# A router and eight experts behind sigmoid attention: the second expert product in row form, one comparison input in PSUM, gathered row blocks turned six transposes at a time

## The chip, the core and the metric

The kernel runs on one core of a Trainium2 chip. A core has five engines that run side by side, each through its own list of instructions in order: TensorE (PE, matrix products and transposes; PEld is its weight load), VectorE (DVE), ScalarE (ACT), GpSimd (POOL) and SyncE (SP, which issues most transfers). TensorE writes only to PSUM, a small accumulator memory of eight banks; the engines wait for each other by semaphores. The metric is device time of one execution in microseconds (us), the median of several runs.

## What is computed

Attention with a sigmoid in place of the softmax, then a layer of eight experts in which each expert takes exactly 448 of the 3584 tokens, chosen greedily by the largest gate values:

```python
def _attn_ref(q, k, v):                      # 8 batches, 12 heads, 448 positions, 64 wide
    scores = scale * np.matmul(q, k.transpose(0, 1, 3, 2)) - np.log(S)
    return np.matmul(1.0 / (1.0 + np.exp(-scores)), v)

def _moe_ref(x, w_gate, w1, w2):             # x: 3584 x 768, 8 experts, hidden 1024
    cap = N // E                             # 448
    order = np.argsort(-(x @ w_gate).flatten())
    for idx in order:
        tok, e = (int(idx) // E, int(idx) % E)
        if assigned[tok] >= 0 or counts[e] >= cap:
            continue
        assigned[tok] = e
        counts[e] += 1
    for e in range(E):
        mask = assigned == e
        out[mask] = np.maximum(x[mask] @ w1[e], 0.0) @ w2[e]
```

All of it is fp32. A product that must keep fp32 accuracy is made of three matmuls: each factor is split into a rounded part (`h`, type fp32r) and the rest (`l`), and the sum takes h x h, h x l and l x h.

## The kernel before

**Stages.** Up to some 276 us the attention runs. To about 327 us the router finds the first expert's tokens while the attention rows `xs` are written to memory. From there the eight experts run one after the other, in the order in which the router finds them full; while one expert is computed, the router (on DVE, with small matmuls on TensorE) finds the tokens of the next.

**One expert** (`moe(kx)`). Its 448 token rows are fetched by an indirect transfer into `xg`, in four row blocks of 128, 128, 128 and 64 (`gather`). Each row block is turned by TensorE so that the model dimension lies on the partitions: two half turns of three 128x128 transposes into a `tp` bank of PSUM, from where ACT makes the rounded part `xh` and DVE the rest `xl` (`xturn`). There are two `tp` buffers.

The first product makes the hidden layer transposed: four blocks `i` of 256 hidden units, each 36 matmuls with 448 moving columns (the tokens) into one `sc` accumulator. An `sc` is two PSUM banks, and there are two of them. ACT reads it twice, as the rounded part `hh` and as fp32 `yt`, and POOL subtracts the two into `hl`.

The second product also comes out transposed: three slices `i` of 256 output columns, each 48 matmuls of 448 columns into one `sc` (L716, L718, L720). A weight block is the stationary operand, the hidden layer moves. ACT copies the result to `yt`, and for each of the four token blocks `untranspose` (L642) turns it back: two transposes into a `tp` bank (L646), a copy of 256 columns into the row buffer `yr` (L651), and after the third slice an indirect transfer on POOL that scatters the rows to `out` (L654). In the last expert the last slice is computed in two cuts of 256 and 192 columns.

**Weights.** `units` lists the weight pieces in order. For each, SP loads `wr`, ACT makes the rounded part `wh` and POOL (for odd pieces from `W_DVE` on, DVE) the rest `wl`. `stream(u)` at the start of piece u issues the load three pieces ahead and the split two ahead. There are four buffers of each.

**What sets the order.** The program is written out in one order by hand: `moe` is a generator that yields after each matmul its estimated cost (`MM` = 189 ns), and the loop around it adds these up in `clock`. When the clock passes a router step's due time the next piece of the router is issued; otherwise, at most every `CHORE_NS` = 1000 ns, the first chore that is due: a gather, a half turn or a back-turn. So the distance between chores is counted in matmuls. What is left at the end of an expert is issued at once (`flush`). The times of the clock decide the order only; each engine then runs its list as its waits allow.

**The router's lists.** `lists` builds from each token's slot number a table of 64 x 32 comparisons a partition (`oh`, L279), which TensorE uses 32 times (L284) to turn slots into token numbers. Both inputs, `io64` and `rr`, are 16-bit integers in SBUF.

## Time and profile before

| what | time |
|---|---|
| median of 3 runs | 883.82 us (882.51 to 1052.58) |
| the profiled execution | 882.62 us |
| its span, from the first instruction to the last | 880.8 us |
| PE busy | 836.0 us (95%) |
| PE weight loads busy | 639.6 us (73%) |
| DVE, ACT, POOL busy | 530.4, 455.3, 467.2 us |
| chain that ended last: PE, DVE, waits on issue | 79%, 10%, 4% |
| transfers | 117.57 MB, mean 133 GB/s |

The profile is of one execution. Its span is 1.8 us shorter than its own time, and that time is close to the lower end of the runs. The chain is the work that ended last, followed back from the last instruction; TensorE's share of it says that the time is mostly a row of its instructions. A row of the timeline gives the start and the length in us, the engine, the line, the operation and what it writes and reads; a row of the groups gives the busy time of all, the mean of one in ns, and the idle time before it with what ended it.

### The profile page before, as it was taken

To read this page: it belongs to the slowest core of one execution; us is meant where nothing else is said; L and a number is where in the kernel's file an instruction comes from. 1 tells how busy PE (TensorE), PEld (TensorE's weight loads), DVE (VectorE), ACT (ScalarE), POOL (GpSimd) and SP (SyncE) were. 2 spreads that over 40 slices of the span, in tenths; PEclk is the share of its full clock that TensorE was granted. 3 is DMA by queue.
4 is the path that set the end of the run, shared out by engine and by line. 5 is a ranking of instruction groups with operands and counts; after the bars stand their busy time and mean duration, and the time that the engine had idled before them with its cause. 6 is when DMAs were issued, how large, how long until landed. Compare 5 with 4: busy or idle time off the path is not lost.

```text
span 880.8 us, 16227 instructions
## 1 busy us (share of the span) xinstructions
PE 836.0 (95%) x5507; PEld 639.6 (73%) x5507; DVE 530.4 (60%) x2045; ACT 455.3 (52%) x611; POOL 467.2 (53%) x449
## 2 busy tenths in 40 slices
PE   6999999999998739998999999999999999999996
PEld 3455455455455629987988988988888888889996
DVE  4665555555555978868779789779699521421110
ACT  6777777777775714334435434434434434544431
POOL 9645444444400025846854964974873882752641
PEclk9999999999999959999999999999999999999998
DMA  9876666666603954334543543452452442722511
GB/s 174 170 142 127 132 124 124 128 127 122 136 19 121 325 178 128 102 115 155 144 135 109 168 138 108 143 161 93 141 165 94 155 147 73 243 98 75 192 48 63
DMA packets 203507, 117.57 MB, mean 133 GB/s; under 512 B 143936, under 2 KB 193088, under 8 KB 203424
## 3 DMA queue, kind: packets, MB, share of 16 engines
q1 hardware_dynamic: 190688, 83.03, 36.0%
q0 software_dynamic: 10880, 33.28, 12.0%
q8 instruction: 43, 0.70, 0.3%
q10 hardware_dynamic: 1856, 0.23, 0.2%
q14 instruction: 40, 0.33, 0.1%
HBM read 94.47 MB, written 22.02 MB: 132 GB/s over the span
## 4 chain that ended last, share of the span: by engine, by line
PE 79%; DVE 10%; issue 4%; POOL 3%; DMA 3%; ACT 0%; ACTq 0%; SPq 0%; POOLq 0%; DVEq 0%
PE tp L462 13%; PE sc L438 11%; PE sc L683 9%; PE sc L681 8%; PE sc L685 8%; PE sc L718 6%; PE sc L720 6%; PE sc L716 6%; DVE r_junk L173 4%; PE tp L468 2%; PE sc L448 2%; PE tp L646 2%; DMA xr<-xs,r_idx 2%; PE tp L633 2%; PE tp L483 1%
## 5 line engine op out<-in xcount | busy, mean ns | idle before, releaser
L599 POOL TENSOR_TENSOR wl<-wr,wh 128x768 fp32r<-128x768 f32 (+1 forms) x96 | 205.8, 2152 | 135.6 <-ACT wh L597 128.3
L428 ACT ACTIVATE at<-sc,bias 128x896 f32<-128x896 f32 x168 | 161.0, 1005 | 63.3 <-PE sc L448 38.4
L373 POOL DMA_DIRECT2D nkq<-in_q_dram x188 | 118.3, 645 | 111.5 <-DVE kqT L413 101.4
L720 PE MATMUL sc<-hh,wl 128*128 128x448 f32 (+2 forms) x400 | 151.4, 379 | 0.0
L685 PE MATMUL sc<-xh,wl 128*128 128x448 f32 (+2 forms) x396 | 146.1, 369 | 0.0
L683 PE MATMUL sc<-xl,wh 128*128 128x448 f32 (+2 forms) x396 | 145.8, 368 | 0.0
L718 PE MATMUL sc<-hl,wh 128*128 128x448 f32 (+2 forms) x400 | 145.5, 364 | 0.1
L681 PE MATMUL sc<-xh,wh 128*128 128x448 f32 (+2 forms) x396 | 144.7, 365 | 0.0
L716 PE MATMUL sc<-hh,wh 128*128 128x448 f32 (+2 forms) x400 | 143.9, 360 | 0.0
L173 DVE TENSOR_SCALAR_CACHE_REDUCE r_junk<-r_KE,r_T 128x224 bf16<-128x224 f32 x315 | 123.2, 441 | 0.1
L462 PE MATMUL tp<-at,nv 128*64 128x448 f32 x576 | 118.6, 547 | 0.0
L597 ACT ACTIVATE wh<-wr 128x768 fp32r<-128x768 f32 (+1 forms) x112 | 102.0, 939 | 13.2 <-DMA wr<-in_moe_w_dram 13.2
L693 POOL TENSOR_TENSOR hl<-yt,hh 128x896 fp32r<-128x896 f32 x32 | 68.3, 2133 | 45.8 <-ACT yt L692 43.1
L422 DVE TENSOR_TENSOR kqL<-kqT,kqH 128x896 fp32r<-128x896 f32 (+1 forms) x49 | 52.5, 1072 | 58.3 <-ACT kqH L420 58.2
L689 ACT ACTIVATE hh<-sc 128x896 fp32r<-128x896 f32 x32 | 29.4, 920 | 111.2 <-PE sc L685 111.2
L619 POOL DMA_INDIRECT xr<-xs,r_idx x32 | 32.5, 1017 | 90.7 <-ACT wh L597 79.8
L718 PEld LDWEIGHTS sc<-hl,wh 128*128 128x128 f32 x400 | 75.2, 188 | 7.1 <-issue 1.1
L599 DVE TENSOR_TENSOR wl<-wr,wh 128x768 fp32r<-128x768 f32 (+1 forms) x16 | 25.0, 1570 | 91.8 <-ACT wh L597 91.8
L462 PEld LDWEIGHTS tp<-at,nv 128*64 128x64 f32 x576 | 37.1, 136 | 59.3 <-issue 57.9
L683 PEld LDWEIGHTS sc<-xl,wh 128*128 128x128 f32 x396 | 75.3, 190 | 6.3 <-issue 0.5
L681 PEld LDWEIGHTS sc<-xh,wh 128*128 128x128 f32 x396 | 75.4, 190 | 5.5
L716 PEld LDWEIGHTS sc<-hh,wh 128*128 128x128 f32 x400 | 75.6, 189 | 4.5
(157 smaller groups left out, 1316.6 us busy)
## 6 DMA issues: line engine op xcount, KB each, us to landing
wr<-in_moe_w_dram SPq DMA_DIRECT2D x64, 384.0 KB, 3.0
wr<-in_moe_w_dram SPq DMA_DIRECT2D x48, 512.0 KB, 3.9
xs<-xr SPq DMA_DIRECT2D x32, 336.0 KB, 4.3
nkq<-in_k_dram SPq DMA_DIRECT2D x190, 56.0 KB, 2.6
nkq<-in_q_dram POOLq DMA_DIRECT2D x188, 56.0 KB, 2.7
nv<-in_v_dram SPq DMA_DIRECT2D x92, 96.0 KB, 2.5
nr<-in_v_dram SPq DMA_DIRECT2D x46, 32.0 KB, 2.3
xr<-xs,r_idx POOLq DMA_INDIRECT x32, 4.6
```

The source lines that it names most:

```text
L173: nc.vector.tensor_scalar(junk, KE, T[:, i:i + 1].bitcast(F32), None, OP.is_ge, OP.add, accum_out=cnt[:, i:i + 1])
L373: qn.dma_start(t[o:o + 32, n], rws[x])
L428: nc.scalar.activation(a, p[:, :, :S], AF.Sigmoid, bias=bias, scale=1 / math.sqrt(D))
L462: nc.tensor.matmul(p[j * 64:j * 64 + 64, :S], nat["v", b, g][:, h0 + j, c, :], AT[b, pr, c][:, j, :], start=(c == 0), stop=(c == 2 and pr ...
L597: nc.scalar.activation(hi, raw[u], AF.Copy)
L599: eng.tensor_tensor(lo, raw[u], hi.bitcast(F32), OP.subtract)
L681: nc.tensor.matmul(ph[:, f, lo:hi], wh[:, a, fs], xh[:, dd, lo:hi], start=st, stop=False)
L683: nc.tensor.matmul(ph[:, f, lo:hi], wh[:, a, fs], xl[:, dd, lo:hi], start=False, stop=False)
L685: nc.tensor.matmul(ph[:, f, lo:hi], wl[:, a, fs], xh[:, dd, lo:hi], start=False, stop=en)
L716: nc.tensor.matmul(py[:, d2, :w], wh[:, a, dsl], h1, start=st, stop=False)
L718: nc.tensor.matmul(py[:, d2, :w], wh[:, a, dsl], h2, start=False, stop=False)
L720: nc.tensor.matmul(py[:, d2, :w], wl[:, a, dsl], h1, start=False, stop=(j == 1 and a == 3))
```

## The change

It has three parts.

1. The second product is computed in row form. A block of 128 tokens of the hidden layer is now the stationary operand, and 384 output columns of the weights move (`W2`), in two halves `i`. For each half there are two open accumulators `py[0]` and `py[1]`, each of two banks: token blocks 0 and 1, and blocks 2 and 3. The result has tokens on the partitions, so `untranspose` and its copies go; `scatter` keeps the indirect transfer. The last 64 tokens have their rounded part and their rest side by side in one stationary block `hr` of 128, so two matmuls do for them what three do for the others; their two partial results come out on partitions 0 to 63 and 64 to 127 and are added by POOL (in the last half by DVE). For this the hidden layer is stored in two pieces, `hb` (384 tokens) and `hr` (64), and ACT reads each `sc` three times. Per half and hidden block there are 3 + 3 + 3 + 2 = 11 matmuls. The weights of the second product come as eight pieces of 2 x 384, with `units` now 16 an expert; `W_DVE` goes from 84 to 96, both the start of the seventh expert. The cut of the last slice is gone.
2. In `lists` the remainder `rr` lies in PSUM as fp32 from the second expert on.
3. The two half turns of a row block are one chore, with 2500 ns between blocks (`TURN_NS`).

```diff
-    def lists(self):
+    def lists(self, alone):
...
-        rr = wk.tile([112, 32], I16, name="r_rr")
+        rr = wk.tile([112, 32], I16, name="r_rr") if alone else P[:, 320:352]
...
-        units = [(kx, st, i, j) for kx in range(E) for st, n in ((0, 4), (1, 3)) for i in range(n) for j in range(2)]
+        units = [(kx, st, i, j) for kx in range(E) for st, n in ((0, 4), (1, 2)) for i in range(n) for j in range(8 // n)]
...
-                h1 = hp.tile([128, 2, S], F32R, name="hh", bufs=4)
-                h2 = hp.tile([128, 2, S], F32R, name="hl", bufs=4)
-                nc.scalar.activation(h1, ph[:, :, :S], AF.Relu)
+                h = hp.tile([128, 2, 2, W2], F32R, name="hb", bufs=4)
+                r = hp.tile([128, 2, 128], F32R, name="hr", bufs=4)
+                parts = ((h[:, :, 0], h[:, :, 1], slice(0, W2)), (r[:, :, :64], r[:, :, 64:], slice(W2, S)))
+                for h1, h2, t in parts:
+                    nc.scalar.activation(h1, ph[:, :, t], AF.Relu)
...
+            yr = [xp.tile([128, 2, DM], F32, name="yr", bufs=YR_BUFS) for _ in range(2)]
+            for i in range(2):
+                cs = slice(i * W2, (i + 1) * W2)
+                py = [ps_s.tile([128, 2, 512], F32, name="sc") for _ in range(2)]
+                for j in range(4):
...
+                    for z in range(2):
+                        for a in range(2):
+                            f = 2 * j + a
+                            h, r = hb[j][0][:, a], hb[j][1][:, a]
+                            st, en = f == 0, f == 7
+                            for c in range(2):
+                                o = py[z][:, c, :W2]
+                                if z == 0 or c == 0:
+                                    t = slice((2 * z + c) * 128, (2 * z + c + 1) * 128)
+                                    terms = ((h[:, 0, t], wh), (h[:, 1, t], wh), (h[:, 0, t], wl))
+                                else:
+                                    terms = ((r, wh), (r, wl))
+                                for n, (hs, w) in enumerate(terms):
+                                    nc.tensor.matmul(o, hs, w[:, a], start=st and n == 0,
+                                                     stop=en and n == len(terms) - 1)
+                                    yield MM2
+                        if j == 3:
+                            last = (kx, i) == (E - 1, 1)
+                            if z == 0:
+                                nc.scalar.copy(yr[0][:, :, cs], py[0][:, :, :W2])
+                            else:
+                                (nc.vector.tensor_copy if last else nc.scalar.copy)(yr[1][:, 0, cs], py[1][:, 0, :W2])
+                                e = hp.tile([64, W2], F32, name="rest", bufs=2)
+                                nc.scalar.copy(e, py[1][64:, 1, :W2])
...
+                                    nc.scalar.copy(yr[1][:64, 1, cs], py[1][:64, 1, :W2])
+                                    nc.gpsimd.tensor_tensor(yr[1][:64, 1, cs], yr[1][:64, 1, cs], e, OP.add)
...
-                    for hf in range(2):
-                        chores.append((t0 + lag + 1500 * j, kx + 1,
-                                       lambda j=j, n=n, hf=hf: xturn(kx + 1, j, n, hf, False)))
+                    chores.append((t0 + lag + TURN_NS * j, kx + 1,
+                                   lambda j=j, n=n: [xturn(kx + 1, j, n, hf, False) for hf in range(2)]))
```

Where the instructions stand is seen at three places. First TensorE in the second product of the first expert, before the change (a row is a line, an operation, what it writes and reads, and the shape of the result; x2 stands for two in a row):

```order
L716 MATMUL sc<-hh,wh 128x448
L718 MATMUL sc<-hl,wh 128x448
L720 MATMUL sc<-hh,wl 128x448
L716 MATMUL sc<-hh,wh 128x448
L718 MATMUL sc<-hl,wh 128x448
L646 MATMUL tp<-ident,yt 128x128 x2
L720 MATMUL sc<-hh,wl 128x448
```

and with the change, one hidden block of the second product on TensorE (blocks 0 and 1, later 2 and the rest block):

```order
L715 MATMUL sc<-wh,hb 128x384 x2
L715 MATMUL sc<-wl,hb 128x384
L715 MATMUL sc<-wh,hb 128x384 x2
L715 MATMUL sc<-wl,hb 128x384
L715 MATMUL sc<-wh,hr 128x384
L715 MATMUL sc<-wl,hr 128x384
```

The transposes L646 between the matmuls are gone, and the matmuls have 384 columns in place of 448.

Second, TensorE at the first change of expert, before the change:

```order
L720 MATMUL sc<-hh,wl 128x448
L633 MATMUL tp<-ident,xr 128x128 x18
L633 MATMUL tp<-ident,xr 128x64 x6
L681 MATMUL sc<-xh,wh 128x448
L683 MATMUL sc<-xl,wh 128x448
```

and with the change, from the second of the four row blocks on (the first stands eleven matmuls earlier):

```order
L715 MATMUL sc<-wh,hb 128x384
L634 MATMUL tp<-ident,xr 128x128 x6
L715 MATMUL sc<-wh,hb 128x384
L715 MATMUL sc<-wl,hb 128x384
L715 MATMUL sc<-wh,hb 128x384 x2
L715 MATMUL sc<-wl,hb 128x384
L715 MATMUL sc<-wh,hr 128x384
L715 MATMUL sc<-wl,hr 128x384
L715 MATMUL sc<-wh,hb 128x384 x2
L715 MATMUL sc<-wl,hb 128x384
L715 MATMUL sc<-wh,hr 128x384
L715 MATMUL sc<-wl,hr 128x384
```

Twelve of the 24 transposes that stood in a row at the end now stand among matmuls; the other twelve follow the last row shown.

Third, ACT from the last block of the first product through the first half of the second, before the change:

```order
L689 ACTIVATE hh<-sc 128x896
L692 ACTIVATE yt<-sc 128x896
L597 ACTIVATE wh<-wr 128x1024 x2
L724 COPY yt<-sc 128x896
L597 ACTIVATE wh<-wr 128x1024
L651 COPY xr<-tp 128x256 x3
```

and with the change:

```order
L683 ACTIVATE hb<-sc 128x2x384
L683 ACTIVATE hr<-sc 128x2x64
L686 ACTIVATE h_4634<-sc 128x896
L598 ACTIVATE wh<-wr 128x768 x4
L721 COPY yr<-sc 128x2x384
L723 COPY yr<-sc 128x384
L725 COPY rest<-sc 64x384
L729 COPY yr<-sc 64x384
```

ACT reads the last `sc` of the first product three times in place of two, straight one after the other, then come four splits, then the four copies of a half's result.

More of the change, by code (lines that the diff above doesn't have):

```diff
@@ L21 @@
 TWO23 = float(2 ** 23)
-XR_BUFS = 12
+XR_BUFS = 8
 XT_BUFS = 8
@@ L25 @@
 AT_BUFS = 8
-YT_BUFS = 3
+YR_BUFS = 3
 LATE_PER_STEP = 2
@@ L31 @@
 CHORE_NS = 1000
+TURN_NS = 2500
 H_POOL = 8
@@ L34 @@
 FIRST = 4000.0
-W_DVE = 84
+W_DVE = 96
 class Consts:
@@ L331, in phase @@
         yield from self.place()
-        yield from self.lists()
+        yield from self.lists(k == 0)
 def moe_attention(tc, q, k, v, w_gate, w1, w2, out):
@@ L579, in load_w @@
                 gate[kx] = nc.sync.value_load(picked[kx][:1, :1], min_val=0, max_val=E - 1)
-            t = wp.tile([128, 1024], F32, name="wr")
+            t = wp.tile([128, 768], F32, name="wr")
             if behind:
@@ L587, in load_w @@
             else:
-                t = t.rearrange("p (a f) -> p a f", a=4)
+                t = t.rearrange("p (a f) -> p a f", a=2)
                 src = w2[ds(gate[kx], 1)].rearrange("e (a p) f -> p (e a) f", p=128)
-                nc.sync.dma_start(t, src[:, 4 * j:4 * j + 4, i * 256:(i + 1) * 256])
+                nc.sync.dma_start(t, src[:, 2 * j:2 * j + 2, i * 384:(i + 1) * 384])
             raw[u] = t
         def split_w(u):
-            n = 3 if units[u][1] == 0 else 4
-            hi = wp.tile([128, 1024], F32R, name="wh")[:, :n * 256].rearrange("p (a f) -> p a f", a=n)
-            lo = wp.tile([128, 1024], F32R, name="wl")[:, :n * 256].rearrange("p (a f) -> p a f", a=n)
+            n = 3 if units[u][1] == 0 else 2
+            hi = wp.tile([128, 768], F32R, name="wh").rearrange("p (a f) -> p a f", a=n)
+            lo = wp.tile([128, 768], F32R, name="wl").rearrange("p (a f) -> p a f", a=n)
             nc.scalar.activation(hi, raw[u], AF.Copy)
@@ L639, in moe_attention, with scatter @@
         scat, chores = [], []
-        MM = 189
-        def untranspose(kx, yr, i, yt, j, n, t0=0, end=False):
-            p = R.bank() if end and j % 2 else ps_t.tile([128, 512], F32, name="tp")
-            for d2 in range(2):
-                nc.tensor.transpose(p[:n, d2 * 128:(d2 + 1) * 128], yt[:, d2, j * 128 - t0:j * 128 - t0 + n], ident)
-            dst = yr[j][:n, i * 256:(i + 1) * 256]
-            if end and j % 2:
-                nc.vector.tensor_copy(dst, p[:n, :256])
-            else:
-                nc.scalar.copy(dst, p[:n, :256])
-            if i == 2:
-                nc.gpsimd.memset(spacer, 0.0)
-                ins = nc.gpsimd.indirect_dma_start(
-                    out=out, out_offset=bass.IndirectOffsetOnAxis(ap=listed[kx][:n, j:j + 1], axis=0),
-                    in_=yr[j][:n], in_offset=None)
-                for o in scat:
-                    tc.declare_no_dep(ins.ins, o.ins, reason="rows of other tokens")
-                scat.append(ins)
+        MM, MM2, W2 = 189, 164, 384
+        def scatter(kx, yr, j, n):
+            nc.gpsimd.memset(spacer, 0.0)
+            ins = nc.gpsimd.indirect_dma_start(
+                out=out, out_offset=bass.IndirectOffsetOnAxis(ap=listed[kx][:n, j:j + 1], axis=0),
+                in_=yr[j // 2][:n, j % 2], in_offset=None)
+            for o in scat:
+                tc.declare_no_dep(ins.ins, o.ins, reason="rows of other tokens")
+            scat.append(ins)
         def moe(kx):
@@ L663, in moe @@
             xh, xl = XH[kx]
-            hh, hl = [], []
+            hb = []
             for i in range(4):
```

58 lines of the change are left out of this document (20 added, 38 removed).

## The prediction

> **What bounds the kernel now.** I read the windows view by stages first, then TensorE's timeline inside the expert stage, then the groups by form, last the waits around the places that the change touches.
>
> ```profile
> core 0 of [0], span 880.8 us
> ...
> 404.00:873.00 469.00, 465.61 (x2614) 413.01 (x2612) 277.85 (x1323) 197.56 (x307) 290.83 (x195) 1.00 0.40 130
> ```
>
> The columns are PE, PE's weight loads, DVE, ACT, POOL, then the granted clock. From 404 us to 873 us TensorE is busy for 465.61 of 469 us at a granted clock of 1.00, while ACT works 197.56 us and POOL 290.83 us. So in this stage the time is TensorE's own list of work: what the change adds there or takes away is the term that counts, and ACT and POOL have room. A busy PE does not say how long one matmul holds it up. That is read from the distance between starts, in three undisturbed stretches and across one pair of transposes:
>
> ```profile
> 535.14 0.37 PE L716 MATMUL sc<-hh,wh 128*128 128x448 f32 x1
> 535.34 0.38 PE L646 MATMUL tp<-ident,yt 128*128 128x128 f32 x2
> 535.48 0.45 PE L718 MATMUL sc<-hl,wh 128*128 128x448 f32 x1
> 535.77 0.37 PE L720 MATMUL sc<-hh,wl 128*128 128x448 f32 x1
> ```
>
> ```profile
> 550.58 0.36 PE L683 MATMUL sc<-xl,wh 128*128 128x448 f32 x1
> ...
> 562.34 0.36 PE L685 MATMUL sc<-xh,wl 128*128 128x448 f32 x1
> ```
>
> ```profile
> 864.29 0.28 PE L716 MATMUL sc<-hh,wh 128*128 128x256 f32 x1
> ...
> 866.56 0.28 PE L718 MATMUL sc<-hl,wh 128*128 128x256 f32 x1
> ```
>
> ```profile
> 868.94 0.27 PE L716 MATMUL sc<-hh,wh 128*128 128x192 f32 x1
> ...
> 872.51 0.27 PE L720 MATMUL sc<-hh,wl 128*128 128x192 f32 x1
> ```
>
> With 448 columns, 58 distances in 562.34 - 550.58 = 11.76 us: 0.2028 us each. With 256 columns, 19 in 2.27 us: 0.1195. With 192 columns, 32 in 3.57 us: 0.1116. From 256 to 448 the cost grows with the columns; from 192 to 256 hardly, so something near 0.11 us (a weight load per matmul) is the floor there. One pair of back-transposes costs 0.63 us less two matmuls (0.406) = 0.224 us.
>
> **The change part by part.**
>
> *More and shorter matmuls (added).* The second product had 144 matmuls of 448 columns an expert, of which the last expert cut 48 in two. So before: 1104 x 0.2028 + 48 x 0.1195 + 48 x 0.1116 = 223.9 + 5.7 + 5.4 = 235.0 us. The row form has, for each of 2 column halves and 8 hidden blocks, 11 matmuls of 384 columns (three full row blocks of three terms, the rest block of two): 176 an expert, 1408 in all. The trace has no 384. Below lies 256 (0.1195), above 448 (0.2028); 384 lies two thirds of the way, and both ends are above the floor, so I take 0.1195 + 128 x 0.0833/192 = 0.1750 us. 1408 x 0.1750 = 246.4 us. This term is **+11.4 us**, on TensorE, with nothing to hide it.
>
> *No back-transposes (removed).*
>
> The code makes 3 slices x 4 blocks x 8 experts = 96 pairs. Two pairs run after the last matmul and belong to the tail. 94 x 0.224 = **-21.1 us**, all in the middle of TensorE's stream. ACT and DVE lose the copies behind them, which were off the path.
>
> *Hand-overs of the accumulators.* The row form keeps two double-bank accumulators open, which are all there are. So its second one must wait until ACT has read the last block of the first product, now in three reads where there were two; and the next half waits for its copies.
>
> ```profile
> 362.97 0.36 PE L685 MATMUL sc<-xh,wl 128*128 128x448 f32 x1
> 363.17 0.37 PE L716 MATMUL sc<-hh,wh 128*128 128x448 f32 x1
> 363.37 0.92 ACT L689 ACTIVATE hh<-sc 128x896 fp32r<-128x896 f32 x1 [3.67 <-PE sc L685]
> 364.18 0.91 ACT L692 ACTIVATE yt<-sc 128x896 f32<-128x896 f32 x1
> ```
>
> ```profile
> L597 ACT ACTIVATE wh<-wr 128x768 fp32r<-128x768 f32 x64 | 52.8, 847 | 13.2 <-DMA wr<-in_moe_w_dram 13.2
> L493 ACT COPY xr<-sc 112x768 f32<-112x768 f32 x32 | 23.9, 802 | 9.6 <-PE sc L491 5.7 <-ACT xr L493 2.8 <-issue 1.1
> L636 ACT ACTIVATE xh<-tp 128x192 fp32r<-128x192 f32 x15 | 5.0, 332 | 9.6 <-PE tp L633 9.3
> ```
>
> ACT starts 0.40 us after the start of the last matmul (362.97 to 363.37), and successive reads start 0.1 us before the one ahead ends (0.92 long, 0.81 apart). Reads of 768, 128 and 896 elements take about 0.80, 0.28 and 0.91 (0.816 ns an element between the 332 ns of 192 and the 802 ns of 768): the last ends near 363.37 + 0.70 + 0.18 + 0.91 = 365.16. TensorE comes to the second accumulator after 12 matmuls, 363.17 + 2.10 = 365.27. Between the two halves the three copies of 384 (0.49 each by the same slope, 0.39 apart) end 0.40 + 1.27 = 1.67 us after the last matmul starts, TensorE arrives after 0.18 + 2.10 = 2.28. At the next expert one copy of 0.80 lies under ten matmuls, 1.75 us. I take **0**; the cover at the first is only 0.1 us, and it is gone as soon as a split `wh` (0.847) stands ahead of the reads. A hand-over can only add, so the bounds are 0 and 24 of them (three an expert) at 0.85 = 20.4 us.
>
> *Six transposes in one go.* They cost TensorE the same as twice three. What changes is where they stand at the first change of expert. Before, all 24 stood there in a row:
>
> ```profile
> 396.50 0.36 PE L720 MATMUL sc<-hh,wl 128*128 128x448 f32 x1
> ...
> 400.69 1.01 PE L633 MATMUL tp<-ident,xr 128*128 128x128 f32 x6 [0.82 <-DVE xl L637]
> 402.41 0.86 PE L633 MATMUL tp<-ident,xr 64*128 64x64 f32 x6 [0.71 <-DVE xl L637]
> 403.62 0.47 PE L683 MATMUL sc<-xl,wh 128*128 128x448 f32 x1
> 403.93 0.36 PE L685 MATMUL sc<-xh,wl 128*128 128x448 f32 x1
> ```
>
> From 396.50 to 403.93 pass 7.43 us; three matmuls take 0.61 and 24 transposes at 0.112 take 2.69, so 4.1 us are waits. Now twelve stand among matmuls and twelve at the end. One round of six is 1.72 us (400.69 to 402.41), the way out 1.2 us (402.41 to 403.62), so the end still waits about 1.5 to 2 us. I take **-2.0**, with bounds 0 (the gathers still late) and -4.1.
>
> *The comparison input in PSUM.*
>
> ```profile
> 505.96 4.75 POOL L599 TENSOR_TENSOR wl<-wr,wh 128x1024 fp32r<-128x1024 f32 x2
> 509.15 2.64 DVE L279 TENSOR_TENSOR r_oh<-c_io,r_rr 112x2048 f16<-112x2048 int16 x1
> 572.26 1.22 DVE L279 TENSOR_TENSOR r_oh<-c_io,r_rr 112x2048 f16<-112x2048 int16 x1
> 574.60 0.64 PE L284 MATMUL rt<-r_oh,c_mv 112*32 112x64 f16 x16
> ```
>
> ```profile
> L165 DVE COPY r_KE<-rt 128x224 f32<-128x224 f32 x7 | 2.7, 390 | 3.5 <-PE rt L162 3.5
> L470 DVE COPY xt<-tp 128x448 f32<-128x448 f32 x47 | 29.3, 624 | 49.7 <-PE tp L468 34.4 <-PE tp L462 15.3
> ```
>
> The comparison takes 1.22 us when left alone, but 2.64 when POOL is in the middle of a split: at 511.79 it ends 1.08 us after POOL does (510.71). Reads from PSUM cost 1.045 ns an element (390 to 624 ns for 224 more), so 2048 take 624 + 1600 x 1.045 = 2.30 us, in seven of the eight (the first expert's stays as it was). TensorE comes for it 1.12 us after its end at 572.26 + 1.22; 1.08 us more just fits, and 25 matmuls of 0.175 instead of 21 of 0.2028 add 0.1. I take 0; bounds -0.4 (the held-up ones no longer late) and 7 x 1.08 = +7.6.
>
> A rule speaks against this edit. The Trainium skill's page "VectorE: DVE Perf Modes" (Why PSUM operands drop a tier; Side-by-side) says that an fp32 operand in PSUM leaves the engine at one element a cycle, 2293 ns for 2048, where 16-bit operands in SBUF reach 1224 ns. The trace agrees with the second (1.22 us) and no run here shows the first; by the page the comparison would be 1.07 us dearer, and the sum the same, since it fits in TensorE's lead. The skill's page "SBUF — State Buffer" (Who interferes with whom) has the other side: a VectorE operation with two SBUF inputs and a GpSimd operation that reads SBUF shut each other out, one with a single SBUF input does not. The held-up 2.64 us agrees; by that rule the sum is 0.4 us lower at most.
>
> *POOL, ACT and the weights.*
>
> ```profile
> wr<-in_moe_w_dram SPq DMA_DIRECT2D x64, 384.0 KB, 3.0
> ```
>
> By the two splits of 1024 above (4.75 us) POOL takes 2.3 ns an element. The change gives it six more small operations an expert, four of 128 elements and two of 384: about 3.0 us, 24 us in all beside 290.83 of 469. ACT loses twelve small copies and three large ones an expert and gains eight copies and four short reads, about even. The weights of the second product come in eight pieces of 384 KB, not six of 512. Such a piece lands in 3.0 us, and one is asked for every 22 x 0.175 = 3.85 us, three pieces ahead. All of it lies beside TensorE's work: 0. If POOL's room were gone, its 24 us would be the price.
>
> *The tail.*
>
> ```profile
> 874.53 0.95 POOL L654 DMA_INDIRECT out_dram<-xr,r_idx  x1 [3.38 <-ACT xr L651]
> 875.79 0.90 POOL L654 DMA_INDIRECT out_dram<-xr,r_idx  x1 [0.23 <-issue]
> ```
>
> From the last matmul (872.51) to the end are 8.3 us, 5.0 of them from the last scatter's start. Now four scatters stand close: the first waits for a copy of 768 that ends 0.5 us before the last matmul starts, and scatters start 1.26 us apart (874.53 to 875.79), so the last starts 0.4 us before plus three times 1.26, 3.4 us after the last matmul: 8.4 us. I take **0**, bounds -1.5 and +1.5.
>
> *Sum.* 11.4 - 21.1 - 2.0 = -11.7. The profiled run's span of 880.8 becomes 869.1. Its own time was 882.62, 1.8 more than its span, so 870.9. That run stands 1.2 below the median of the runs shown, 883.82; against it this is -1.5%.
>
> **The rivals.**
>
> - *Hand-overs become waits (slower).* At each of the 24 hand-overs a split `wh` stands ahead of ACT's reads: 870.9 + 20.4 = 891.3. It is slower than the median before from 12.9/24 = 0.54 us each. For it: 0.1 us of cover. Against: the order puts the three reads straight after the first product's last matmul, with the splits behind. 0.10.
> - *A weight load bounds the shorter matmul (slower).* If a load takes as long as its record, 0.19 us, 1408 x 0.19 = 267.5, 21.1 more: 892.0. Against: at 256 columns one goes through in 0.1195. 0.05.
>
> ```profile
> L716 PEld LDWEIGHTS sc<-hh,wh 128*128 128x128 f32 x400 | 75.6, 189 | 4.5
> PEld tp L633 <- DVE xl L637: 10.1, 18, 1.7
> ```
>
> - *The turns' waits go too (faster by more).* Transposes waited 10.1 us for DVE to clear their bank. If six in one go, further apart, end 5 of these beside the 2 counted, and the first change of expert is free (2.1 more): 863.8. 0.20.
> - *The slower comparison makes the lists late,* the one-element rate as a mechanism of this kernel: if DVE lags there, each of seven costs 1.08: 878.5. The page on VectorE names this rate. 0.06.
>
> **How the numbers follow.** My forecast, 866 to 876, has 0.55; the rivals 0.10, 0.05, 0.20 and 0.06; 0.04 is left for what I don't see, half of it on either side. The predicted time is 870.9. The range 861 to 884 takes in the extra gain and the slow comparison, and leaves out at most 0.19 above and below. Faster by over 2% (about what a measurement of this kernel can tell from no change) means below 866.1: 0.20 + 0.02 = 0.22. Slower by over 2%, above 901.5, is the other 0.02. Within: 0.76.
>
> **What would show it.** The matmuls of 384 columns start 0.175 us apart; 0.19 or more proves the weight load. No transposes of `yt` are left. TensorE stays above 99% busy from 404 us on; a gap before the 13th matmul of a second product, released by ACT, proves the hand-over. The comparison takes 2.3 us, all alike, and no wait of TensorE follows it. At the first change of expert twelve transposes wait under 2.5 us. If an expert's second product does not shorten from 29.2 + 2.7 to 30.8 us, the forecast is wrong in its main term.

## The result, and the profile after

The changed kernel took 875.62 us (median of 4 runs, 874.18 to 876.93), the kernel before 884.04 us on the same chip. The ratio is 0.9906, with a 95% interval of 0.9888 to 0.9924: 0.9% faster, where 1.5% was forecast, and inside the forecast range. A second set of runs on another occasion gave 0.9908 (0.9879 to 0.9938). The profiled execution took 874.18 us, its span is 872.4 us (880.8 before). The medians take in two single runs that were far slower than the rest (1052.58 us among the four before, 1653.54 us among the ten of one experiment); the ratios leave them out.

First the same windows view as before, from 404 us to the last matmul; columns as there.

```profile
404.00:864.00 460.00, 453.07 (x2611) 421.26 (x2609) 276.65 (x1302) 179.92 (x293) 302.65 (x243) 1.00 0.41 130
```

TensorE still sets the time, at the full granted clock. But it is now busy for 453.07 of 460 us (98.5%), not 465.61 of 469 (99.3%): the stage has 6.9 us of gaps where it had 3.4. Next come stretches of TensorE's timeline, two of the first product and then one of the second (start, duration, instruction).

```profile
340.75 0.36 PE L675 MATMUL sc<-xl,wh 128*128 128x448 f32 x1
...
360.81 0.36 PE L675 MATMUL sc<-xl,wh 128*128 128x448 f32 x1
...
469.79 0.37 PE L675 MATMUL sc<-xl,wh 128*128 128x448 f32 x1
...
491.90 0.37 PE L673 MATMUL sc<-xh,wh 128*128 128x448 f32 x1
...
845.82 0.33 PE L715 MATMUL sc<-wl,hb 128*128 128x384 f32 x1
...
857.96 0.33 PE L715 MATMUL sc<-wh,hb 128*128 128x384 f32 x1
```

384 columns: 70 distances in 12.14 us, 0.1734 us each (0.1740 over all 1407). 448 columns: 99 distances in 20.06 us at the start of the stage, 0.2027 each as before; but from 470 us on 107 distances in 22.11 us, 0.2067 each. That longer spacing was not in the forecast. Then TensorE's waits (total, times, longest), and the group of the comparison.

```profile
PE tp L634 <- DVE xl L638: 6.2, 4, 2.2
PE tp L634 <- DMA xr<-xs,r_idx: 6.0, 1, 6.0
PE rt L285 <- DVE r_oh L280: 3.4, 1, 3.4
...
PE sc L677 <- POOL wl L600: 1.4, 1, 1.4
PE sc L715 <- POOL wl L600: 0.3, 1, 0.3
```

```profile
L280 DVE TENSOR_TENSOR r_oh<-c_io,rt 112x2048 f16<-112x2048 int16 x7 | 15.9, 2276 | 0.0
```

The 3.4 us for `r_oh` and the 6.0 us for `xr` belong to the first expert and stood there before. New are 1.7 us for `wl` on GpSimd, and 6.2 us for `xl` on VectorE where it was 3.1. The comparison from PSUM takes 2.28 us, seven times alike. The page "VectorE: DVE Perf Modes" of the Trainium skill (Side-by-side) gives 2293 ns for it; the trace agrees.

I added up the distances between TensorE's starts by what stands between them, from the first matmul of the expert stage to the last (us). A matmul counts with its undisturbed distance, and what a distance has beyond that goes to what stands in it:

| part of TensorE's stream | before | after | difference | forecast |
|---|---|---|---|---|
| second product | 235.4 | 244.9 | +9.5 | +11.4 |
| back-transposes and the search's matmuls | 41.3 | 20.3 | -21.0 | -21.1 |
| turns with their waits | 30.0 | 28.9 | -1.0 | -2.0 |
| first product, 448 columns | 226.5 | 228.8 | +2.3 | 0 |
| waits for `wl` on GpSimd | 0.2 | 2.0 | +1.8 | 0 |
| last matmul to the end | 8.3 | 8.5 | +0.2 | 0 |

That is -8.2 us, against -8.4 in the span. Read this way, the forecast was off by small sizes alone. The experiments tell another story: what each edit is worth does not add up like this.

### The profile page after: what moved, and what is told of

It is laid out like the page before. It is cut to its first block, busy times and chain, and to the rows that moved or that the text cites. A ratio compares the mean times of both kernels' runs of the same rounds, so it can differ in the third digit from the quotient of the medians.

```text
span 872.4 us, 16402 instructions
## 1 busy us (share of the span) xinstructions
PE 823.4 (94%) x5523; PEld 650.5 (75%) x5523; DVE 533.9 (61%) x2047; ACT 437.9 (50%) x602; POOL 485.5 (56%) x510
## 4 chain that ended last, share of the span: by engine, by line
PE 80%; DVE 11%; POOL 3%; issue 2%; DMA 2%; SPq 1%; ACT 0%; ACTq 0%; POOLq 0%; DVEq 0%
PE sc L715 22%; PE tp L463 13%; PE sc L439 11%; PE sc L675 8%; PE sc L673 8%; PE sc L677 8%; DVE r_junk L174 4%; PE tp L469 3%; PE sc L449 2%; PE tp L634 2%; PE tp L484 1%; POOL out_dram L646 1%; POOL xr L620 1%; PE rt L285 1%; POOL wl L600 1%
## 5 line engine op out<-in xcount | busy, mean ns | idle before, releaser
L600 POOL TENSOR_TENSOR wl<-wr,wh 128x768 fp32r<-128x768 f32 x110 | 202.3, 1853 | 32.3 <-ACT wh L598 32.0
L715 PE MATMUL sc<-wh,hb 128*128 128x384 f32 x768 | 200.4, 339 | 0.0
L715 PEld LDWEIGHTS sc<-wh,hb 128*128 128x128 f32 x768 | 138.1, 188 | 1.8 <-issue 0.7
L715 PE MATMUL sc<-wl,hb 128*128 128x384 f32 x384 | 129.5, 337 | 0.3 <-POOL wl L600 0.3
L598 ACT ACTIVATE wh<-wr 128x768 fp32r<-128x768 f32 x128 | 104.1, 851 | 51.0 <-PE sc L715 30.7
L683 ACT ACTIVATE hb<-sc 128x768 fp32r<-128x768 f32 x32 | 26.0, 814 | 142.4 <-PE sc L677 142.4
L689 POOL TENSOR_TENSOR hb<-h,hb 128x768 fp32r<-128x768 f32 x32 | 59.2, 1850 | 49.9 <-ACT h L686 46.7
L600 DVE TENSOR_TENSOR wl<-wr,wh 128x768 fp32r<-128x768 f32 x18 | 23.8, 1329 | 96.9 <-ACT wh L598 96.8
L677 PEld LDWEIGHTS sc<-xh,wl 128*128 128x128 f32 x396 | 75.0, 189 | 8.2 <-POOL wl L600 1.7
L715 PEld LDWEIGHTS sc<-wl,hb 128*128 128x128 f32 x384 | 72.1, 188 | 0.8 <-POOL wl L600 0.6
```

The costliest lines, as they stand in the source:

```text
L598: nc.scalar.activation(hi, raw[u], AF.Copy)
L600: eng.tensor_tensor(lo, raw[u], hi.bitcast(F32), OP.subtract)
L677: nc.tensor.matmul(ph[:, f, lo:hi], wl[:, a, fs], xh[:, dd, lo:hi], start=False, stop=en)
L689: nc.gpsimd.tensor_tensor(h2, h0[:, :, t], h1.bitcast(F32), OP.subtract)
L715: nc.tensor.matmul(o, hs, w[:, a], start=st and n == 0, stop=en and n == len(terms) - 1)
```

## The experiments

**One edit at a time.** Three edits make seven combinations. Six were run, all against the kernel before, each with its own runs of it.

*The row form alone* (the changed kernel with the comparison and the turns as before):

```diff
-        yield from self.lists(k == 0)
+        yield from self.lists(True)
-                    chores.append((t0 + lag + TURN_NS * j, kx + 1,
-                                   lambda j=j, n=n: [xturn(kx + 1, j, n, hf, False) for hf in range(2)]))
+                    for hf in range(2):
+                        chores.append((t0 + lag + 1500 * j, kx + 1,
+                                       lambda j=j, n=n, hf=hf: xturn(kx + 1, j, n, hf, False)))
```

> The row form alone: every comparison reads its input from SBUF as before, and the turns are two chores of three transposes, 1500 ns apart, as before. Theory A (the row form carries the result; the other two edits are worth little): the second product costs 9.5 us more and the back-transposes 21.0 less, the first product 2.3 more, as in the changed kernel; without the turn's edit 1 us of the gain is missing: 876.5, between 875 and 878. Theory B (the other two edits eat part of the gain): 870 to 873. Theory C (the other two bring a good part of the measured gain): 879 or more.

*Without the turns in one go* has only the second half of that diff:

> The changed kernel with the turns as before: two chores of three transposes, 1500 ns apart. The turn chunks of the changed kernel cost 28.95 us of TensorE's stream where the kernel before had 29.99, so theory A says 1 us slower than the changed kernel, 876 to 877.5. Theory B (six in one go put waits of 0.95 to 2.5 us into the later changes of expert, which two of three would not have): 3 to 5 us faster, 871 to 873. Theory C, the prediction's: 2 us slower, with most of it at the first change of expert, where 24 transposes stood with 4.1 us of waits.

*Without the comparison in PSUM* has only the first half:

> The changed kernel with the comparison's input in SBUF for all eight lists: seven comparisons go from 2.277 us back to 1.22 when left alone, and to about 2.6 where GpSimd is in the middle of a split. Theory A (they lie in TensorE's lead): the time stays, within 0.5 us of the changed kernel. Theory B (the slower comparison makes the turns behind it wait on VectorE): up to 7 x 1.06 = 7.4 us faster, and the waits of tp for xl get shorter by about 1 us each. Theory C (the held-up ones were the late ones): up to 1 us slower.

*The comparison in PSUM alone*, in the kernel before:

```diff
-        rr = wk.tile([112, 32], I16, name="r_rr")
+        rr = wk.tile([112, 32], I16, name="r_rr") if alone else P[:, 320:352]
```

> The kernel before with the comparison's input in PSUM for lists 1 to 7, and nothing else. In the kernel before two comparisons were late, by 0.03 and 0.35 us, and the six others lay 0.64 us or more ahead of TensorE. Theory A (the edit is worth what the row form's denser GpSimd work costs the comparison, and little without it): at most 0.4 us faster than the kernel before, and not over 0.5 slower. Theory B (it is worth the same in either kernel): 4 to 6 us faster.

*The turns in one go alone*, in the kernel before:

```diff
-                    for hf in range(2):
-                        chores.append((t0 + lag + 1500 * j, kx + 1,
-                                       lambda j=j, n=n, hf=hf: xturn(kx + 1, j, n, hf, False)))
+                    chores.append((t0 + lag + 2500 * j, kx + 1,
+                                       lambda j=j, n=n: [xturn(kx + 1, j, n, hf, False) for hf in range(2)]))
```

> The kernel before with its turns as six transposes in one go, 2500 ns apart, and nothing else. Its 24 transposes at the first change of expert stay in one row. The two turns of 64 rows cost 0.52 us each when three stand alone and 0.72 for six, so seven changes of expert save 7 x 0.32 = 2.3 us. Theory A (that is all): 2 to 2.5 us faster than the kernel before. Theory B (the prediction's 2.0 was for the first change of expert alone, and without the row form it isn't there, and three cost half of six): no change. Theory C (it is worth 3.8 us, as in the row form): 3.5 to 4 us faster.

What was measured:

| row form | comparison in PSUM | turns in one go | us | ratio to before, 95% interval |
|---|---|---|---|---|
| x | | | 884.63 | 1.0012 (0.9996 to 1.0028) |
| | x | | 883.49 | 1.0010 (0.9996 to 1.0024) |
| | | x | 886.51 | 1.0038 (1.0022 to 1.0055) |
| x | x | | 879.44 | 0.9959 (0.9947 to 0.9972) |
| x | | x | 881.45 | 0.9970 (0.9953 to 0.9986) |
| x | x | x | 875.62 | 0.9906 (0.9888 to 0.9924) |

No edit alone gains anything; one costs 0.4%. Together they gain 0.9%. The lone ratios add up to +0.6%, so 1.5%, some 13.5 us, lies in how the edits act on each other (comparison and turns without the row form were not run). Of the expectations only two came out: that for the comparison alone at theory A (0.8 us slower where at most 0.5 was said, but the interval takes in no change), and that for the row form alone at theory C. With the comparison taken back the time is some 6 us worse than that of the changed kernel, with the turns taken back 4 to 5, and the turns alone make the kernel before slower; no theory had these sizes.

*Why the comparison matters only with the row form.* Timeline of the changed kernel without the comparison in PSUM, at the first list (VectorE, GpSimd and TensorE):

```profile
379.94 1.01 POOL L730 TENSOR_TENSOR yr<-yr,rest 64x384 f32<-64x384 f32 x1 [5.94 <-ACT yr L729]
...
380.61 4.98 DVE L280 TENSOR_TENSOR r_oh<-c_io,r_rr 112x2048 f16<-112x2048 int16 x1
...
380.91 3.61 POOL L600 TENSOR_TENSOR wl<-wr,wh 128x768 fp32r<-128x768 f32 x2
...
385.65 1.09 PE L285 MATMUL rt<-r_oh,c_mv 112*32 112x64 f16 x32 [2.54 <-DVE r_oh L280]
```

and the same place in the changed kernel:

```profile
380.62 2.28 DVE L280 TENSOR_TENSOR r_oh<-c_io,rt 112x2048 f16<-112x2048 int16 x1
...
380.90 3.64 POOL L600 TENSOR_TENSOR wl<-wr,wh 128x768 fp32r<-128x768 f32 x2
...
383.03 1.12 PE L285 MATMUL rt<-r_oh,c_mv 112*32 112x64 f16 x32
```

The addition `yr<-yr,rest` is one of the small GpSimd operations that the row form brings, and two splits follow it without a gap. GpSimd had been idle for 5.94 us ahead of it, waiting for ACT. ACT's timeline there shows why the three come together: the copies of the half's result stand ahead of the roundings `wh` that the splits need.

```profile
379.39 0.47 ACT L729 COPY yr<-sc 64x384 f32<-64x384 f32 x1
379.76 1.58 ACT L598 ACTIVATE wh<-wr 128x768 fp32r<-128x768 f32 x2
```

In the kernel before, GpSimd's timeline has its splits near this place one by one, with 1.88 us of idle time between them:

```profile
375.04 2.40 POOL L599 TENSOR_TENSOR wl<-wr,wh 128x1024 fp32r<-128x1024 f32 x1 [3.00 <-ACT wh L597]
379.33 2.39 POOL L599 TENSOR_TENSOR wl<-wr,wh 128x1024 fp32r<-128x1024 f32 x1 [1.88 <-ACT wh L597]
```

In the row form the comparison with both inputs in SBUF starts beside the three and ends 1.07 us after the last of them (380.91 + 3.61 = 384.52; 385.59): it does nearly all of its work, which alone takes 1.22 us, when GpSimd has stopped. It takes 4.98 us, and TensorE stands idle for 2.54. With one input in PSUM it takes 2.28 us whatever GpSimd does, and TensorE starts 0.13 us after it with no wait on record. Over the eight lists TensorE's stretches with the search's matmuls cost 25.2 us in the first kernel and 20.3 in the second, 4.9 less. Of these, 4.1 us are waits for the comparison at three lists (2.54, 0.30 and 1.30 us); the rest is mostly matmuls at half the clock behind the first wait, of which more below. The row form alone has the same waits; its line, of which some 3.5 us are again the first expert's, is:

```profile
PE rt L285 <- DVE r_oh L280: 7.6, 4, 3.5
```

In the kernel before, the comparisons take up to 3.01 us, but TensorE comes later for most of them: two were late, by 0.3 us at most; hence the edit is worth nothing there (1.0010). The page "SBUF — State Buffer" of the Trainium skill (Who interferes with whom) has the rule: two SBUF inputs on VectorE and a GpSimd read of SBUF exclude each other. The trace agrees, and shows VectorE kept out by GpSimd operations in succession. It need not come so: in the same trace, at the third list, two splits follow each other without a gap too, and there the comparison got in between them (2.74 us; the second split took 2.85 us where the others take 1.84). What decides this no run shows. Nor did a run take the additions, or the order of ACT's copies, back alone: that they are what crowds GpSimd is read from the timelines.

*Why the turns in one go need the row form.* TensorE's timeline in the kernel before with the turns in one go, and a line of its waits there:

```profile
526.40 0.82 PE L633 MATMUL tp<-ident,xr 128*128 128x128 f32 x6
...
529.27 0.44 PE L646 MATMUL tp<-ident,yt 128*128 128x128 f32 x2 [0.83 <-DVE xl L637]
```

```profile
PE tp L646 <- DVE xl L637: 3.0, 4, 0.9
```

A turn in one go takes both `tp` banks. There a back-transpose is next in line, needs one of them, and waits until VectorE has cleared it. By the count of the table above the turns got 1.2 us shorter (30.0 to 28.8), the stretches with back-transposes or the search's matmuls some 6 us longer. But some 4 us of these sums are matmuls at half the clock, in a stretch of 6.8 us at the first change of expert and one of 3.4 us at the second, where the trace of the kernel before has none. At the full clock the turns are some 3 us shorter and the back-transposes some 3.5 us longer, so that the edit would be worth about nothing; most of what this trace lost is the clock. That it is not this one execution alone is seen from the mean granted clock of the runs, 0.981 in the median here and 0.984 in the kernel before: at most 0.003 of 886 us, 2.7 us by estimate, of the 3.4 that the edit costs.

In the row form there are no back-transposes, and nobody is behind the turn. Then the gain is partly one that the forecast had denied. TensorE's timeline without the turns in one go, and in the changed kernel, at a block of 64 rows:

```profile
724.18 0.34 PE L715 MATMUL sc<-wl,hb 128*128 128x384 f32 x1
724.45 0.40 PE L634 MATMUL tp<-ident,xr 64*128 64x64 f32 x3
724.78 0.62 PE L715 MATMUL sc<-wh,hb 128*128 128x384 f32 x2
```

```profile
717.08 0.34 PE L715 MATMUL sc<-wl,hb 128*128 128x384 f32 x1
717.35 0.58 PE L634 MATMUL tp<-ident,xr 64*128 64x64 f32 x6
717.86 0.62 PE L715 MATMUL sc<-wh,hb 128*128 128x384 f32 x2
```

From matmul to matmul pass 0.60 us with three transposes and 0.78 with six. With the longer distance behind them they cost 0.53 and 0.72 us, so two turns of three cost 0.34 us more than one of six: 2.4 us over seven changes of expert. For blocks of 128 rows it is not so: there three transposes cost 0.33 us and six 0.66. All turns together cost 33.6 us of TensorE's stream without the edit (and 1.5 us of matmuls at half the clock) and 28.9 with it; the other 2.3 us are mostly shorter waits for `xl` (7.8 us without the edit, 6.2 with it).

*What a wait costs besides itself.* The windows view of the changed kernel without the comparison in PSUM, around the wait of 2.54 us, and of the changed kernel:

```profile
383.00:387.00 4.00, 1.46 (x34) 1.24 (x34) 2.80 (x2) 0.34 (x1) 1.51 (x1) 0.90 0.64 195
387.00:389.70 2.70, 2.70 (x10) 2.25 (x10) 0.83 (x5) 0.00 (x0) 0.44 (x1) 0.52 0.01 3
```

```profile
383.00:387.00 4.00, 4.00 (x50) 3.48 (x50) 1.70 (x7) 0.34 (x1) 2.51 (x2) 1.00 0.62 191
387.00:389.70 2.70, 2.70 (x16) 2.39 (x14) 2.53 (x6) 0.00 (x0) 2.59 (x2) 1.00 0.73 190
```

Behind the wait the granted clock is 0.52 for 2.7 us, and 10 matmuls go where 16 went. Such stretches, each 3.4 us long, stand behind waits of 2.0 to 2.5 us in this trace three times, and cost 3.1 us in all; some of it is in the 4.9 us above. This is part of why the two edits are worth more in the time than their waits: the mean granted clock of the runs is 0.981 in the median without the comparison in PSUM and 0.984 in the changed kernel.

**The first product's spacing.** One transpose of the identity ahead of each first product from the third expert on, into a bank that nobody reads:

```diff
             xh, xl = XH[kx]
             hb = []
+            if kx > 1:
+                nc.tensor.transpose(ps_t.tile([128, 512], F32, name="tp")[:, :128], ident, ident)
```

> The changed kernel with one more transpose of the identity, 128x128, into a bank that nobody reads, ahead of the first product of experts 2 to 7; nothing else. Matmuls of 448 columns start 202.7 ns apart in some stretches and 206.7 in others; in the changed kernel the first products of experts 2 to 7 run at 206.7 and follow straight on matmuls of 384 columns, while that of expert 1 follows on transposes and runs at 202.7. Theory A (which spacing holds is set by what stands right ahead, and a transpose sets it to the short one): all first products run at 203, 6 x (144 x 4 ns - 0.2) = 2.3 us faster than the changed kernel, 873.3. Theory B (the long spacing comes from what goes on beside, such as transfers or a clock): the spacings stay as they were, and the time is 0.5 to 1.3 us longer.

Measured: 876.61 us, ratio 0.9922 (0.9901 to 0.9944), no gain. TensorE's timeline:

```profile
340.82 0.37 PE L679 MATMUL sc<-xh,wl 128*128 128x448 f32 x1
...
360.87 0.37 PE L675 MATMUL sc<-xh,wh 128*128 128x448 f32 x1
...
473.83 0.36 PE L675 MATMUL sc<-xh,wh 128*128 128x448 f32 x1
...
493.89 0.36 PE L675 MATMUL sc<-xh,wh 128*128 128x448 f32 x1
```

From 473.83 us on 99 distances take 0.2027 us each, where the changed kernel had 0.2067; so it went at the start of five of the six first products with a transpose ahead. The last stayed at 0.2067. And the first two experts, where nothing was changed, went from 0.2027 to 0.2067 (97 distances in 20.05 us). The average fell from 205.0 to 204.4 ns only, and the six transposes cost 0.7 us. What picks the spacing stays open.

**The changed kernel again:**

> The changed kernel unaltered, beside the others on one chip: 874 to 877. Theory A (the spread is two states of TensorE's stream, drawn anew in each execution): its trace has stretches of 448 columns at 206.7 ns in other places than the first trace had, and, where a wait of 2 us or more stands, perhaps a stretch of about ten matmuls at half the clock. Theory B: it repeats the first trace stretch by stretch.

875.54 us. Its first products average 205.0 ns as before, but behind the wait at the first change of expert it has seven matmuls at half the clock, 1.2 us, which the first trace lacks. So that stretch comes and goes between executions of one kernel.

**The hand-over to the second product.** A fourth read of the accumulator by ACT:

```diff
                     nc.scalar.activation(h0, ph[:, :, :S], AF.Relu)
+                    if i == 3:
+                        nc.scalar.activation(hp.tile([128, 2, S], F32, name="more", bufs=1), ph[:, :, :S], AF.Relu)
```

> The changed kernel with a fourth read by ACT, of 896 elements and about 0.8 us, of the last accumulator of each first product, into a tile that nobody uses. The prediction gave the hand-over to the second product 0.1 us of cover. Theory A (the cover is that small): TensorE waits some 0.7 us ahead of the 13th matmul of each of the eight second products, 5.6 us in all, released by ACT. Theory B (the cover is 0.8 us or more): no such wait, and the time of the changed kernel within 1 us.

One run, 880.63 us. Timeline of ACT, then of TensorE, at the first hand-over:

```profile
363.32 0.93 ACT L686 ACTIVATE h<-sc 128x896 f32<-128x896 f32 x1
364.12 0.94 ACT L688 ACTIVATE more<-sc 128x896 f32<-128x896 f32 x1
...
364.19 0.34 PE L717 MATMUL sc<-wl,hb 128*128 128x384 f32 x1
365.11 0.61 PE L717 MATMUL sc<-wh,hb 128*128 128x384 f32 x2 [0.58 <-ACT more L688]
```

The read adds 0.80 us to ACT's row, and the 13th matmul comes 0.92 us after the one ahead, 0.75 late. The cover was 0.05 us. The distances grow by 4.3 us over the eight hand-overs: 0.75 us at five of them, 0.4 at one, almost nothing at two, where other work of TensorE stands ahead of the 13th matmul. That is theory A, with 5.6 us forecast.

**GpSimd's row of gathers and scatters.** GpSimd's timeline in the changed kernel at the last change of expert (from the last scatter to the late split), and TensorE's:

```profile
747.11 0.91 POOL L646 DMA_INDIRECT out_dram<-yr,r_idx  x1 [0.22 <-issue]
748.32 0.98 POOL L620 DMA_INDIRECT xr<-xs,r_idx  x1 [0.30 <-issue]
...
750.88 1.11 POOL L620 DMA_INDIRECT xr<-xs,r_idx  x1 [0.30 <-issue]
752.02 1.85 POOL L689 TENSOR_TENSOR hb<-h,hb 128x768 fp32r<-128x768 f32 x1
...
754.23 1.81 POOL L600 TENSOR_TENSOR wl<-wr,wh 128x768 fp32r<-128x768 f32 x1
...
756.09 0.47 PE L677 MATMUL sc<-xh,wl 128*128 128x448 f32 x1 [1.35 <-POOL wl L600]
```

```diff
-                    chores.append((t0 + 1500 * j, kx + 1, lambda j=j, n=n: gather(kx + 1, j, n)))
+                    chores.append((t0 + (4000 + 3000 * j if lag > 12000 else 1500 * j), kx + 1, lambda j=j, n=n: gather(kx + 1, j, n)))
```

> The changed kernel with the four gathers 3000 ns apart, from 4000 ns on, where the turns have time (the late experts), not 1500 apart from 0 on. In the changed kernel TensorE waits 0.5 us and 1.5 us for a split that GpSimd is late with, because four scatters and three gathers stand ahead of it in one stretch. Theory A (that row on GpSimd is the cause): both waits go, 2 us faster than the changed kernel, 873.5. Theory B (GpSimd has no room at those places in any order): the waits move and the time stays.

874.18 us, ratio 0.9894 (0.9851 to 0.9936). The waits for `wl` are gone from the trace, as theory A has it. The time is 1.4 us lower, less than the interval can tell from nothing; this trace has a half-clock stretch, worth 1.5 us, which the first trace of the changed kernel lacks.

**The turns' waits for VectorE.** The timeline of the changed kernel at the second change of expert:

```profile
455.57 2.22 DVE L207 TENSOR_SCALAR r_T<-c_kk,r_J 128x3 int32<-128x3 int32 x1
455.92 1.84 POOL L600 TENSOR_TENSOR wl<-wr,wh 128x768 fp32r<-128x768 f32 x1
457.71 1.01 DVE L638 TENSOR_TENSOR xl<-tp,xh 128x384 fp32r<-128x384 f32 x2
458.30 1.01 PE L634 MATMUL tp<-ident,xr 128*128 128x128 f32 x6 [1.42 <-DVE xl L638]
```

The copies that clear the first turn's banks stand behind steps of the search on VectorE. One of these steps, of three elements, takes 2.22 us beside a split (elsewhere in this trace 0.23 us at the least), and the next turn waits. The first of three tries to keep the two apart holds the search where the late turns stand:

```diff
...
+                    c = next((c for c in chores if c[0] <= t and c[2] in turns), None)
+                    if c:
+                        chores.remove(c)
+                        c[2]()
+                        t_route, t_chore = t + 1100, t + CHORE_NS
+                    else:
+                        t_route = t + next(route, 0) + SLACK
...
```

> The changed kernel with a turn issued only where the next step of the search is due, which is put off by 1100 ns, so that no step of the search stands on VectorE ahead of the copies that clear the turn's bank; turns 3300 ns apart. In the changed kernel the turns' waits for those copies come to 1.8, 0.95 and 2.3 us after the first change of expert, and 2.5 at it. Theory A (VectorE's queue is what is late): 5 us faster than the changed kernel, 870 to 872, and turn chunks of 0.66 us everywhere after the first change. Theory B (the search is put off and its own waits grow by as much): no change, with longer waits for the lists or for the gathered rows.

873.11 us, ratio 0.9876 (0.9852 to 0.9900), beside 0.9908 of the changed kernel in the same set: 2.4 us better, half of what theory A said. The turns fell from 28.9 to 25.4 us, with the waits for `xl` from 6.2 to 3.6. But this trace also has a half-clock stretch, worth 1.5 us, and a first product at 206.4 ns, 1.5 us more. The second try holds the first two changes of expert too:

```diff
+                    chores.append((t0 + (3300 + 1700 * j if kx < 2 else lag + 3300 * j), kx + 1, turn_block))
```

> The run with the turns held, made complete: at the first two changes of expert too a turn goes ahead of a step of the search that is due (from 3300 ns on, 1700 apart, the search put off by 800 each time), so that the turns no longer end in a row of twelve. Theory A (VectorE's queue in front of the turn's copies is what is left): the chunks of 4.4 us at the first and 2.4 us at the second change become chunks of 0.66 us, 3 to 5 us faster than the run with the later turns held, 868.5 to 870.5, and no stretch at half the clock stands behind the first change. Theory B (the gathered rows come late for turns moved forward): TensorE waits there for the gathers instead, and the gain is under 1 us.

872.77 us, ratio 0.9874 (0.9832 to 0.9916): no better than the first. The half-clock stretch is gone, but the turns moved ahead waited 1.0 us for their gathered rows and still 4.0 us for VectorE, with steps of the search ahead of the copies again. So the gain is theory B's, but its cause is so only in part. The third keeps them apart everywhere, with the gathers of the last change spaced:

```diff
-                    chores.append((t0 + 1500 * j, kx + 1, lambda j=j, n=n: gather(kx + 1, j, n)))
+                    chores.append((t0 + (4000 + 3000 * j if lag > 12000 else 1500 * j), kx + 1, lambda j=j, n=n: gather(kx + 1, j, n)))
+                    chores.append((t0 + (3800 + 1700 * j if kx < 6 else lag + 3300 * j), kx + 1, turn_block))
...
+                        t_route, t_chore = t + (1700 if kx < 6 else 1100), t + CHORE_NS
```

> The changed kernel with its turns and its search kept apart: at changes of expert 1 to 6 the four turns come 3800, 5500, 7200 and 8900 ns after the list, ahead of any step of the search, which stands still for 1700 ns after each; at the last change the gathers are 3000 ns apart and the turns 3300, put ahead of a due step. Theory A (what is left of the loss is VectorE's search steps in front of the turns' copies, and GpSimd's row of gathers and scatters): turn chunks of 0.66 to 0.72 us everywhere, 7 us off the 29 of the changed kernel, 2 us of waits for GpSimd's splits gone, and no half-clock stretch behind the first change: 866 to 868. Theory B (each turn moved ahead meets its gathered rows late, as in the run before, or VectorE falls behind): 870 to 873.

870.73 us (869.44 to 871.75), ratio 0.9853 (0.9836 to 0.9871): faster than both kernels, 13 us below the kernel before and some 5 below the changed one. Its waits:

```profile
PE tp L634 <- DMA xr<-xs,r_idx: 11.2, 9, 5.8
...
PE tp L634 <- DVE xl L638: 1.4, 1, 1.4
```

The waits for VectorE fell from 6.2 to 1.4 us, and none for GpSimd's splits is on record where there were 1.7 us (theory A); the gathered rows now come late, 11.2 us where it was 6.0 (theory B). Theory B's time is right. By the count of the table the turns with their waits are no cheaper than in the changed kernel, some 31 us for 28.9. What this trace saves stands elsewhere: some 2.5 us in the stretches with the search's matmuls, 1.7 us in late splits, 1.1 us in matmuls at half the clock at the start of the expert stage, and 0.9 us in the first product's spacing. Turns later by about as much as the rows are late would be the next thing to try; that was not run.

## Why the prediction was right or wrong

- **More and shorter matmuls:** right in kind, 1.9 us too dear. The line between 256 and 448 columns gave 0.1750 us for 384, the trace has 0.1740, which is 1.5 us over 1408; the other 0.4 is that the second product before was 235.4, not 235.0.
- **No back-transposes:** right, -21.0 for -21.1. The main term was sound, and a weight load did not bound the shorter matmul.
- **Hand-overs:** right at 0, no wait of a 13th matmul for ACT is on record in the changed kernel. The cover of 0.1 us was 0.05 where it was measured. The rival was one read away.
- **Six transposes in one go:** two steps failed. "They cost TensorE the same as twice three" is wrong for blocks of 64 rows: 0.72 us against twice 0.53. And -2.0 at the first change of expert was 1.1 (24 transposes in 6.8 us, then in 5.7; the last wait is 2.24 us, forecast 1.5 to 2). At later changes waits for `xl` ate what six in one go saved. Added to the rest of the change the edit is worth 4 to 5 us, and in the kernel before it costs 3.4 (0.38%), in its trace mostly by the half clock, for which the prediction has no term.
- **The comparison in PSUM:** 2.30 us was right, 2.28 measured, and so was that it just fits. TensorE starts 0.05 to 0.16 us after its end; 0.05 also passes where a wait for it is on record, so 0 to 0.1 us are left, and at three of the seven lists nothing. The value, 0 with a gain of 0.4 at most, was wrong. It was bounded by the comparisons of the kernel before, and the row form changes those: without PSUM the same seven take 1.3 to 4.98 us. Taking this edit back costs some 6 us.
- **POOL, ACT and the weights:** this is the step that failed. "All of it lies beside TensorE's work: 0" holds for GpSimd's own results but for 1.7 us of late splits. It left out whom GpSimd keeps from working meanwhile. The row form sets small operations and splits on GpSimd in rows that can shut VectorE's comparison out for longer. The forecast of the row form alone, 11.4 - 21.1 = -9.7 us, came out as +1.1. By the count of the table its trace has some 5 us more than the kernel before in the search's stretches, which is this step; 3.5 us more in the first product's spacing and 2.6 us more in the turns, 1.5 of them at half the clock, make up most of the rest.
- **The first product:** taken as untouched, it cost 2.3 us more, by its spacing; the cause is open.
- **The signs:** TensorE above 99% busy from 404 us on did not come, it was 98.5%; the turns' waits for `xl` and the late splits are what is missing. Twelve transposes with under 2.5 us of wait at the first change of expert came (2.24).
- **The tail:** right, 8.3 to 8.5 us.

So the sum of -11.7 came near the measured -8.4 by luck, because two errors cancelled: the row form was credited with 10.8 us that it does not bring alone, and the other two edits with some 7 us too little: they take away what the row form does to VectorE, and need it in turn to be worth anything.

## What to carry to other kernels

When work is added to GpSimd beside a full TensorE, look not only at whether GpSimd has room but at which VectorE operations with two SBUF inputs run beside it, and what waits for those; an operand in PSUM costs them about twice the time (here 2.28 us for 1.22) and frees them of that. Price edits that touch the same buffers or the same engine together: here each alone was worth nothing or less, and a bound taken from the kernel before was no bound for the changed one. And count a wait of TensorE of 2 us or more, or shorter ones close together, at its length plus the half-clock stretch that may stand behind it.

## What the runs showed of the hardware

- A wait of TensorE of 2.0 to 2.5 us is often followed by 3.4 us at a granted clock of 0.50, which cost 0.6 to 1.5 us each. The same kernel had it behind the same wait of 2.24 us in one execution and not in another. In the kernel before with the turns in one go, waits of 0.71 and 0.84 us close together were enough, and at the first change of expert the stretch was 6.8 us. The page "TensorE: Matmul & The Clock Gate" of the Trainium skill (What's actually happening) tells of a free-running window of about 3.4 us, and of the clock at half after an idle one. That the stretches are 3.4 us long, once twice that, and come and go agrees; but here TensorE had been idle for only 1.2 to 2.5 us of the 3.4 ahead of such a stretch.
- Matmuls of 448 columns run at one of two spacings, 202.7 or 206.7 ns, for tens of microseconds each. The average was 202.8 to 203.0 in the three kernels with the old second product and 204.1 to 206.4 in those with the row form. With a transpose ahead five of six started at the short one, but in the same run the first two experts, with nothing changed, went to the long one; the cause is not known.
- Going from matmuls to transposes of 64 rows and back costs some 0.34 us beside the transposes (an estimate from two sizes): three cost 0.53 us, six 0.72. With 128 rows three cost 0.33 and six 0.66.
- A VectorE operation of three elements, 0.23 us at the least, took 2.22 us beside a GpSimd split of 1.84.
